# Joining two column-split pieces of a chunk on TensorE, from the fifth chunk on, with the instruction order planned anew

## The chip, the cores and the metric

The kernel runs on one core of a Trainium2 chip. The metric is the device time of one execution in microseconds (us), taken as the median of several runs. TensorE (PE in the profile) does the matrix products, VectorE (DVE) and ScalarE (ACT) the elementwise work and the copies out of PSUM, SyncE (SP) issues the transfers.

## The reference

Three steps follow each other; only their shapes and formulas matter here.

```python
# q, k, v, a_re, a_im: batch 4, 8 heads, 768 tokens, head size 48
for t in range(S):                       # a gated linear recurrence
    S_re, S_im = ar*S_re - ai*S_im + kv, ar*S_im + ai*S_re
    y[:, :, t] = einsum('bhd,bhde->bhe', q[:, :, t], S_re)
...
x = y as 3072 tokens x 384
h = x @ w_in; x = (h * clip(h + 3, 0, 6) / 6) @ w_out        # 384 -> 2048 -> 384
h = ((x @ w1) * (x @ w2)) @ w3; return h @ w_out2            # 384 -> 1024 -> 1024 -> 384
```

## The kernel before, in words

The recurrence is done in 24 chunks of 128 tokens, six for each of the four batch entries; `u` counts them from 0. Two chunks make a group, whose gates, angles and scaled keys and queries are prepared by ScalarE and VectorE (`group`). Four chunks (two in each of the first two cases) make a block of 512 tokens (256), and for each block the first network's two layers run on TensorE: `s1` (lines 742 to 744 with output `x`, nine matmuls of 512 columns each for one slice of 128 hidden units) and `s2` (the same lines with output `m`). After the last block come the folding of two weights (lines 1042 to 1044) and the second network.

One chunk (`chunk`) issues on TensorE:

- `tr`, two times three transposes (line 684), whose results ScalarE copies into the tile `Ks`. The first chunks of a batch entry and the later ones alike do this, but the last chunk of a batch entry (u = 5, 11, 17, 23) doesn't, as nobody needs the state after it;
- `sc`, two times four products of keys with queries (line 693), masked by VectorE into the tiles `P0` and `P1`;
- `pv`, the products of V with the masked scores (line 705) and, except in the first chunk of a batch entry, of the state `A` with the queries (line 710), into the PSUM tile `py`, which ScalarE copies to `ys`. `ys` goes by transfers into `xf` and is split by ScalarE (`xh`) and VectorE (`xl`) into the input of `s1`;
- `upd`, the products of V with `Ks` (line 722), into the PSUM tile `pt`, copied by ScalarE to `ut`. It is left out in the last chunk of a batch entry;
- `turned_`, four transposes of `ut` (line 731), after which VectorE forms the next state `A` in two steps (one in the first chunk of a batch entry).

`pv` and `upd` use the array in two halves of 64 columns (`tile_position=(0, 64 * j)`, shown as 128\*64 and 96\*64 in the profile). All other matmuls use it whole. In the traces each of these float32 products counts as two matmul instructions, so `upd` is 16 of them, `pv` 16 in the first chunk of a batch entry and 32 in the others.

Nothing is ordered by hand. Every step is handed to a planner (`Plan`) with an estimated duration, what it reads and writes, and for some steps a due time (`pins`). The planner works the due times backwards (`o.due`), then simulates the engines: whichever engine is free first takes, among its steps whose inputs and buffers are ready, the one due earliest. The order that comes out is the program's order on each engine. Buffers are few: one `Ks`, one `Kc`, one each of `KT`, `QT`, `P0`, `P1`, and five PSUM slots named `x`, shared by `tr`, `sc`, `pv`, `upd`, `turned_` and the outputs of `s1`. `xh` and `xl` exist once, so the next block's input can be written only after the last `s1` of the block before. `FILL`, `UB`, `MB`, `hold` and other constants were set for the order before and stay as they are.

Of the kernel before, what the change touches and what calls it, by code (L numbers as in the profile page):

```python
# [45 lines left out]


class Op:
    __slots__ = ("i", "eng", "dur", "fn", "deps", "succ", "due", "bufs", "end", "table", "nd", "ready", "pin", "lat", "boost", "size", "until")


class Plan:
# [21 lines left out]
        self.slots.setdefault(tag, n)  # L74
        return Buf(tag, make, free, key)

    def add(self, eng, dur, fn, r=(), w=(), table=None, pin=None, lat=None, part=False, boost=0.0, size=0, until=None):
        o = Op()
        o.size, o.until = size, until
        o.i, o.eng, o.dur, o.fn, o.table, o.pin, o.boost = len(self.ops), eng, dur, fn, table, pin, boost + self.bias  # L80
        o.lat = self.LAT if lat is None else lat
        deps = set()
        for b in r:
            deps.update([] if b.part else b.writers)
        for b in w:
            deps.update(b.readers if not b.part else [])
            if not part and not b.part:
                deps.update(b.writers)
        for b in r:
            b.readers.append(o)  # L90
        for b in w:
            if part or b.part:
                b.writers.append(o)
            else:
                b.writers, b.readers = [o], []
        o.bufs = list(dict.fromkeys([b for b in list(r) + list(w) if b.tag is not None]))
        for b in o.bufs:
            b.left += 1
        o.deps, o.succ = deps, []
        for d in deps:  # L100
            d.succ.append(o)
        self.ops.append(o)
        return o

    def run(self, swap, engines=("PE", "ACT", "DVE", "SP", "POOL"), window=48, switch=1.3, hold=4.0, first=None):
        ops = self.ops
        for o in reversed(ops):
            late = o.pin if o.pin is not None else 1e9
# [14 lines left out]
        freed = {t: [] for t in self.slots}  # L123
        held = set()
        table, bus, cols = first, 0.0, {}
        if first:
            swap(first)
        order = []
# [28 lines left out]
        while len(order) < n:  # L157
            e = min((x for x in engines if lists[x]), key=lambda x: free[x])
            now = free[e]
            for o in [x for x in lists[e][:400] if x.until is not None and now >= x.until]:  # L160

                lists[e].remove(o)
                o.end = now
                n -= 1
                done.add(o)
                for b in o.bufs:
                    b.left -= 1
                    if b.left == 0 and b in held:
                        freed[b.tag].append(now + 0.37)
                        freed[b.tag].sort()  # L170
                        bisect.insort(events, now + 0.37)
            if not lists[e]:
                continue
            best, bk, soon = None, None, None
            cnt = 0
            for o in lists[e]:
                if cnt >= window and best is not None:
                    break
                cnt += 1
                if any(d not in done for d in o.deps):  # L180
                    continue
                at = fits(o, now)
                if at is None:
                    continue
                for d in o.deps:
                    at = max(at, d.end + self.gap(d, o))
                key = o.due - o.boost
                if o.table and o.table != table:
                    key += hold
                if at > now + 1e-9:  # L190
                    if soon is None or at < soon:
                        soon = at
                    continue
                if bk is None or key < bk:
                    best, bk = o, key
            if best is None:
                at = bisect.bisect_right(events, now + 1e-9)
                nxt = events[at] if at < len(events) else None
                if soon is not None and (nxt is None or soon < nxt):
                    nxt = soon  # L200
                if nxt is None:
                    parked.add(e)
                    if len(parked) == sum(1 for x in engines if lists[x]):
                        raise RuntimeError("no instruction can go on")
                    free[e] = 1e9
                else:
                    free[e] = nxt
                continue
            o = best
            lists[e].remove(o)  # L210
            if o.table and o.table != table:
                now += switch
                swap(o.table)
                table = o.table
            o.end = now + o.dur
            if e == "PE":
                left, t0 = o.dur, now
                while left > 1e-9:
                    k = int(t0 / TICK + 1e-9)
                    rate = 1.0 if cols.get(k - 1, 0) >= 3060 else 0.5  # L220
                    d = min(left / rate, (k + 1) * TICK - t0)
                    cols[k] = cols.get(k, 0) + d * rate * 2400
                    left -= d * rate
                    t0 += d
                o.end = t0
            for x in parked:
                free[x] = o.end
            parked.clear()
            bisect.insort(events, o.end)
            for g in {self.gap(o, x) for x in o.succ}:  # L230
                bisect.insort(events, o.end + g)
            if o.size:
                bus = max(bus, o.end + 0.65) + o.size / 300e3
                o.lat = bus + 1.55 - o.end
            free[e] = o.end
            for b in o.bufs:
                if b not in held:
                    held.add(b)
                    if b.key:
                        pos[b.key] += 1  # L240
                    if taken[b.tag] < self.slots[b.tag]:
                        taken[b.tag] += 1
                    else:
                        freed[b.tag].pop(0)
                b.left -= 1
                b.end = max(b.end, o.end + (o.lat if o.lat > 1 else 0.0))
                if b.left == 0:
                    at = b.end + (0.37 if b.tag.startswith("ps") else self.LAT)
                    freed[b.tag].append(at)
                    freed[b.tag].sort()  # L250
                    bisect.insort(events, at)
            done.add(o)
            order.append(o)
            o.fn()


def c_act(n, psum=False):
    return n / 1200.0 + (0.05 if psum else 0.095)
# [161 lines left out]
def main_kernel(tc, q, k, v, a_re, a_im, w_in, w_out, w1, w2, w3, w_out2, consts, qT, kT, arT, aiT, vT, wiT, woT, w1T, w2T, w3T, wo2T, out, blocks=(2, 2, 4, 4, 4, 4, 4)):  # L420
# [12 lines left out]
    for n in blocks:  # L433
        blk.append((u0, n))
        u0 += n
    GT = 2
    FILL = (20, 38.1, 10, 52.8, 16, 52.7)
    FIRST_GROUPS = ((0, 2), (2, 2), (4, 2))
    groups = [(b, c0, n) for b in range(B) for c0, n in (FIRST_GROUPS if b == 0 else ((0, 2), (2, 2), (4, 2)))]
# [5 lines left out]
    with tc.tile_pool(name="keep", bufs=1) as kp:  # L445
      c5_ = kp.tile([128, 2, 128], F32, name="c2")
      flag = kp.tile([1, 1], I32, name="flag")
      with ctx:
# [44 lines left out]
        def ACT(dur, fn, r, w, **kw):  # L493
            return P.add("ACT", dur, fn, r, w, **kw)
# [4 lines left out]
        def PE(dur, fn, r, w, **kw):  # L499
            return P.add("PE", dur, fn, r, w, **kw)  # L500
# [4 lines left out]
        def A(o, i, f, scale=1.0, bias=0.0, **kw):  # L505
            act.activation(out=o, in_=i, func=f, scale=scale, bias=bias, **kw)  # L506
# [161 lines left out]
        def chunk(u, c_, Kc, KT, QT, ys, mt):  # L668
# [32 lines left out]
            def pv():  # L701
                for p in range(4):
                    for j in range(2):
                        h = 2 * p + j
                        pe.matmul(py()[64 * j:64 * j + 64, p, :], vb.ap[:, h, :], Pm[h // 4]()[:, h % 4, :],  # L705
                                  start=True, stop=first, tile_position=(0, 64 * j), skip_group_check=True)
                    if not first:
                        for j in range(2):
                            h = 2 * p + j
                            pe.matmul(py()[64 * j:64 * j + 64, p, :], Ap.ap[:, h, :], QT()[:, h, tok],  # L710
                                      start=False, stop=True, tile_position=(0, 64 * j), skip_group_check=True)
            PE(0.1 + 4 * 0.22 * (1 if first else 2), pv, [vb, QT] + Pm + ([] if first else [Ap]), [py, seen[u]])
            ACT(c_act(512, True), lambda: A(ys()[:, :, c_, :], py(), AF.Copy), [py], [ys], part=True)
            if not last:

                pt = PS("x", [128, 4, 96], 5, 1)
# [2 lines left out]
                def upd():  # L719
                    for p in range(4):  # L720
                        for j in range(2):
                            pe.matmul(pt()[64 * j:64 * j + 64, p, :], vb.ap[:, 2 * p + j, :], Ks()[:, 2 * p + j, :],
                                      start=True, stop=True, tile_position=(0, 64 * j), skip_group_check=True)
                PE(4 * 0.17 + 0.02, upd, [Ks, vb], [pt])
                ACT(c_act(384, True), lambda: A(ut(), pt(), AF.Copy), [pt], [ut])
                pu = PS("x", [96, H, 64], 5, 1)
                An = At[u % 2]
# [488 lines left out]
```

## Time and profile before

| | |
|---|---|
| median of three runs | 925.55 us (924.24 to 926.18) |
| the profiled execution's own time | 924.97 us |
| its span, first to last instruction | 922.8 us |
| PE busy | 880.2 us (95%) |
| DVE busy, ACT busy | 586.0 us (63%), 508.8 us (55%) |
| mean granted TensorE clock | 0.998 of full speed |

The span is 2.2 us shorter than the execution's own time. TensorE first works at 27.82 us, when the first group's keys are ready, and is busy for nine tenths or more of each of the page's 40 slices of the span from the fourth to the last but one.

### The profile page before, as it was taken

Reading aid. Unit: us, or ns where it says so; the run is one execution under the profiler, and the core shown is the slowest. Engines: PE = TensorE matmul, PEld = TensorE weight load, DVE = VectorE, ACT = ScalarE, POOL = GpSimd, SP = SyncE. Lnnn points to the kernel's source line nnn. Section 1 sums busy time; section 2 is a strip of 40 time slices with the busy share of each in tenths; the row PEclk is TensorE's granted clock in tenths of the full one; section 3 lists DMA queues with packets and bytes.
Section 4 is the critical chain, followed back from the end, with each engine's and each line's share of the span. In section 5 each row is a group of like instructions: output and inputs, shape, how many; then the busy total and the mean of one; then the engine's idle time right before and its main releaser. Section 6 shows DMA issues by size and latency. Waiting matters only on the chain.

```text
span 922.8 us, 13306 instructions
## 1 busy us (share of the span) xinstructions
PE 880.2 (95%) x5194; PEld 759.2 (82%) x5194; DVE 586.0 (63%) x913; ACT 508.8 (55%) x816; POOL 0.2 (0%) x4
## 2 busy tenths in 40 slices
PE   0689999999999999999999999999999999999997
PEld 0578989888888888878888888898989888898987
DVE  6999999889998787869453699663223232313131
ACT  7999888978887567656523566453222222212130
POOL 0000000000000000000000000000000000000000
PEclk9999999999999999999999999999999999999999
DMA  6894736357581645365325666230101000000001
GB/s 267 214 251 157 197 107 169 96 128 169 159 208 47 152 145 149 81 143 160 98 47 126 204 234 247 92 92 23 60 9 52 18 21 26 5 32 0 35 1 38
DMA packets 55991, 102.88 MB, mean 111 GB/s; under 512 B 6384, under 2 KB 34160, under 8 KB 55920
## 3 DMA queue, kind: packets, MB, share of 16 engines
q1 hardware_dynamic: 55920, 101.94, 38.8%
q8 instruction: 43, 0.70, 0.3%
q14 instruction: 28, 0.23, 0.1%
HBM read 64.62 MB, written 13.63 MB: 85 GB/s over the span
## 4 chain that ended last, share of the span: by engine, by line
PE 75%; ACT 11%; DVE 11%; DMA 1%; issue 1%; SPq 1%; ACTq 0%; DVEq 0%
PE x L742 12%; PE x L743 12%; PE x L744 12%; PE m L742 5%; PE m L743 5%; PE m L744 5%; PE m L1112 4%; PE x L693 4%; PE m L1110 4%; PE m L1111 4%; ACT u L506 3%; ACT W L506 3%; ACT L1146 2%; PE x L705 2%; DVE gl L509 1%; PE x L710 1%
## 5 line engine op out<-in xcount | busy, mean ns | idle before, releaser
L506 ACT ACTIVATE r<-x 128x512 f32<-128x512 f32 (+1 forms) x144 | 82.1, 571 | 88.4 <-PE x L744 64.6
L506 ACT ACTIVATE gh<-r 128x512 fp32r<-128x512 f32 (+1 forms) x108 | 64.2, 596 | 98.1 <-PE m L744 68.5
L742 PE MATMUL m<-gh,W 128*128 128x512 f32 (+1 forms) x288 | 110.1, 382 | 0.5 <-ACT gh L506 0.5
L743 PE MATMUL m<-gl,W 128*128 128x512 f32 (+1 forms) x288 | 107.7, 374 | 1.1 <-DVE gl L509 1.0
L744 PE MATMUL m<-gh,W 128*128 128x512 f32 (+1 forms) x288 | 107.2, 372 | 0.0
L509 DVE TENSOR_TENSOR gl<-r,gh 128x512 fp32r<-128x512 f32 (+1 forms) x108 | 70.0, 648 | 52.3 <-ACT gh L506 50.9
L509 DVE TENSOR_TENSOR r<-r,x 128x512 f32<-128x512 f32 x48 | 33.0, 688 | 103.0 <-PE x L744 103.0
L742 PE MATMUL x<-xh,W 128*128 128x512 f32 x240 | 96.3, 401 | 0.0
L743 PE MATMUL x<-xl,W 128*128 128x512 f32 x240 | 93.7, 390 | 0.0
L744 PE MATMUL x<-xh,W 128*128 128x512 f32 x240 | 93.6, 390 | 0.0
L742 PE MATMUL x<-W 128*128 128x512 f32 (+1 forms) x228 | 84.6, 371 | 0.0
L744 PE MATMUL x<-W 128*128 128x512 f32 (+1 forms) x228 | 83.6, 367 | 0.0
L743 PE MATMUL x<-W 128*128 128x512 f32 (+1 forms) x228 | 83.6, 367 | 0.0
L881 DVE SCALAR_TENSOR_TENSOR r<-r,x 128x512 f32<-128x512 f32 (+1 forms) x96 | 61.0, 637 | 13.0 <-ACT r L506 12.5
L506 ACT ACTIVATE W<-W 128x768 f32<-128x768 f32 (+3 forms) x78 | 64.5, 848 | 5.1 <-DMA W<-in_w3T_dram 2.5
L743 PEld LDWEIGHTS m<-gl,W 128*128 128x128 f32 x288 | 54.3, 188 | 11.3 <-DVE gl L509 2.5
L742 PEld LDWEIGHTS m<-gh,W 128*128 128x128 f32 x288 | 54.2, 188 | 11.0 <-issue 0.9
L744 PEld LDWEIGHTS m<-gh,W 128*128 128x128 f32 x288 | 54.2, 188 | 9.5
L742 PEld LDWEIGHTS x<-xh,W 128*128 128x128 f32 x240 | 45.1, 188 | 10.2 <-issue 0.9
L744 PEld LDWEIGHTS x<-xh,W 128*128 128x128 f32 x240 | 45.1, 188 | 9.7
L743 PEld LDWEIGHTS x<-xl,W 128*128 128x128 f32 x240 | 45.1, 188 | 8.5
L506 ACT ACTIVATE u<-u 128x768 f32<-128x768 f32 x60 | 50.3, 838 | 0.4
(233 smaller groups left out, 1867.0 us busy)
## 6 DMA issues: line engine op xcount, KB each, us to landing
KT<-Kc SPq DMA_DIRECT2D x72, 129.0 KB, 3.6
QT<-cs SPq DMA_DIRECT2D x72, 128.0 KB, 4.6
W<-in_w3T_dram SPq DMA_DIRECT2D x16, 512.0 KB, 4.3
v<-in_vT_dram SPq DMA_DIRECT2D x24, 256.0 KB, 2.8
W<-in_wiT_dram SPq DMA_DIRECT2D x8, 768.0 KB, 6.8
W<-in_woT_dram SPq DMA_DIRECT2D x8, 768.0 KB, 6.5
ar<-in_arT_dram SPq DMA_DIRECT2D x12, 384.0 KB, 3.4
ai<-in_aiT_dram SPq DMA_DIRECT2D x12, 384.0 KB, 3.3
```

Source lines behind the costliest of these rows:

```text
L506: act.activation(out=o, in_=i, func=f, scale=scale, bias=bias, **kw)
L509: dve.tensor_tensor(out=o, in0=i0, in1=i1, op=op)
L693: pe.matmul(p_()[:, i, :], KT()[:, 4 * g + i, tok], QT()[:, 4 * g + i, tok])
L705: pe.matmul(py()[64 * j:64 * j + 64, p, :], vb.ap[:, h, :], Pm[h // 4]()[:, h % 4, :], start=True, stop=first, tile_position=(0, 64 * j), ...
L742: pe.matmul(o, wh, xh, start=start, stop=False, **kw)
L743: pe.matmul(o, wh, xl, start=False, stop=False, **kw)
L744: pe.matmul(o, wl, xh, start=False, stop=stop, **kw)
L881: DVE(c_tt(n), lambda: dve.scalar_tensor_tensor(out=r()[:, :n], in0=r()[:, :n], scalar=6.0, in1=h()[:, :n], op0=ALU.min, op1=ALU.mult), [h ...
L1110: pe.matmul(o(), g[1]()[:, a], Wb()[:, 0, i % 2], start=(i == 0), stop=False)
L1111: pe.matmul(o(), g[1]()[:, a], Wb()[:, 1, i % 2], start=False, stop=False)
L1112: pe.matmul(o(), g[2]()[:, a], Wb()[:, 0, i % 2], start=False, stop=(i == KI - 1))
L1146: P.run(lambda t_: act.preload_act_table_set(t_), window=48, hold=3.94, first=EXP_SET)
```

## The change

From the fifth chunk on (`JOINED = 4`), and where the chunk has an `upd`, `pv` and `upd` are added to the plan as one step of TensorE whose duration is the sum of both and which reads and writes what both do. That holds for 16 chunks: u = 4, 6 to 10, 12 to 16 and 18 to 22. The matmuls themselves stay as they were. The copy of `py` is now added after the step with `upd` in program text. The planner also learns a cost: whenever TensorE goes from a step in halves (`cols=True`) to one with the whole array or back, its simulated clock is charged `turn=0.17` us. As both alter the simulation, the order of all engines is set anew.

```diff
-    def add(self, eng, dur, fn, r=(), w=(), table=None, pin=None, lat=None, part=False, boost=0.0, size=0, until=None):
+    def add(self, eng, dur, fn, r=(), w=(), table=None, pin=None, lat=None, part=False, boost=0.0, size=0, until=None, cols=False):
...
             if e == "PE":
-                left, t0 = o.dur, now
+                left, t0 = o.dur + (turn if o.cols != halves else 0.0), now
+                halves = o.cols
...
+    JOINED = 4
...
-            PE(0.1 + 4 * 0.22 * (1 if first else 2), pv, [vb, QT] + Pm + ([] if first else [Ap]), [py, seen[u]])
-            ACT(c_act(512, True), lambda: A(ys()[:, :, c_, :], py(), AF.Copy), [py], [ys], part=True)
+            pvd, pvr, pvw = 0.1 + 4 * 0.22 * (1 if first else 2), [vb, QT] + Pm + ([] if first else [Ap]), [py, seen[u]]
+            if last or u < JOINED:
+                PE(pvd, pv, pvr, pvw, cols=True)
...
-                PE(4 * 0.17 + 0.02, upd, [Ks, vb], [pt])
+                if u < JOINED:
+                    PE(4 * 0.17 + 0.02, upd, [Ks, vb], [pt], cols=True)
+                else:
+                    PE(pvd + 4 * 0.17, lambda: (pv(), upd()), pvr + [Ks], pvw + [pt], cols=True)
+            ACT(c_act(512, True), lambda: A(ys()[:, :, c_, :], py(), AF.Copy), [py], [ys], part=True)
+            if not last:
                 ACT(c_act(384, True), lambda: A(ut(), pt(), AF.Copy), [pt], [ut])
```

## Rows read from the trace of the kernel before

**Rows 1.** Busy time by stretch: start:end, length, then each engine's busy us.

```profile
0.00:64.00 64.00, 30.74 (x215) 24.49 (x216) 54.08 (x83) 57.35 (x80) 0.20 (x4) 1.00 0.80 247
64.00:169.00 105.00, 102.62 (x830) 93.19 (x830) 101.88 (x166) 94.16 (x158) 0.00 (x0) 1.00 0.59 157
169.00:258.00 89.00, 88.76 (x569) 73.79 (x569) 82.78 (x128) 73.71 (x116) 0.00 (x0) 1.00 0.58 145
258.00:917.00 659.00, 657.89 (x3586) 567.69 (x3584) 346.64 (x538) 283.54 (x466) 0.00 (x0) 1.00 0.30 87
```

**Rows 2.** Timeline of TensorE, an update alone: start, duration, line, operation.

```profile
291.26 0.40 PE L744 MATMUL m<-gh,W 128*128 128x512 f32 x1
291.59 0.88 PE L722 MATMUL x<-Ks,v 128*64 128x96 f32 x16
292.40 0.50 PE L742 MATMUL x<-xh,W 128*128 128x512 f32 x1
292.73 0.39 PE L743 MATMUL x<-xl,W 128*128 128x512 f32 x1
```

**Rows 3.** Timeline of TensorE, an update right behind products with V.

```profile
284.13 0.39 PE L744 MATMUL m<-gh,W 128*128 128x512 f32 x1
284.45 1.09 PE L705 MATMUL x<-P,v 128*64 128x128 f32 x16
285.37 0.83 PE L722 MATMUL x<-Ks,v 128*64 128x96 f32 x16
286.13 0.50 PE L742 MATMUL x<-xh,W 128*128 128x512 f32 x1
286.47 0.40 PE L743 MATMUL x<-xl,W 128*128 128x512 f32 x1
```

**Rows 4.** Timeline of TensorE, products with V alone.

```profile
410.05 0.40 PE L744 MATMUL x<-xh,W 128*128 128x512 f32 x1
410.37 1.09 PE L705 MATMUL x<-P,v 128*64 128x128 f32 x16
411.40 0.50 PE L742 MATMUL m<-gh,W 128*128 128x512 f32 x1
411.73 0.39 PE L743 MATMUL m<-gl,W 128*128 128x512 f32 x1
```

**Rows 5.** Timeline of TensorE, updates and a product with V at other places.

```profile
104.76 0.88 PE L722 MATMUL x<-Ks,v 128*64 128x96 f32 x16
...
204.55 0.83 PE L722 MATMUL x<-Ks,v 128*64 128x96 f32 x16
...
421.04 0.44 PE L705 MATMUL x<-P,v 128*64 128x128 f32 x4
...
452.47 0.88 PE L722 MATMUL x<-Ks,v 128*64 128x96 f32 x16
...
466.78 0.88 PE L722 MATMUL x<-Ks,v 128*64 128x96 f32 x16
...
501.06 0.83 PE L722 MATMUL x<-Ks,v 128*64 128x96 f32 x16
```

**Rows 6.** Timelines of TensorE and ScalarE, from chunk 22 to chunk 23.

```profile
499.25 0.44 PE L705 MATMUL x<-P,v 128*64 128x128 f32 x4
...
501.27 0.60 ACT L506 ACTIVATE ys<-x 128x512 f32<-128x512 f32 x1 [3.47 <-PE x L710]
501.93 0.49 ACT L506 ACTIVATE ut<-x 128x384 f32<-128x384 f32 x1
...
506.33 0.44 PE L705 MATMUL x<-P,v 128*64 128x128 f32 x4
```

**Rows 7.** Timelines of TensorE and VectorE, passage to the last block.

```profile
510.45 0.40 PE L742 MATMUL m<-gh,W 128*128 128x512 f32 x1
...
518.17 0.96 DVE L509 TENSOR_TENSOR xl<-xf,xh 128x768 fp32r<-128x768 f32 x1
...
520.66 0.39 PE L742 MATMUL x<-xh,W 128*128 128x512 f32 x1
```

More of the change, by code (lines that the diff above doesn't have):

```diff
@@ L48 @@
 class Op:
-    __slots__ = ("i", "eng", "dur", "fn", "deps", "succ", "due", "bufs", "end", "table", "nd", "ready", "pin", "lat", "boost", "size", "until")
+    __slots__ = ("i", "eng", "dur", "fn", "deps", "succ", "due", "bufs", "end", "table", "nd", "ready", "pin", "lat", "boost", "size", "until", "cols")
 class Plan:
@@ L75, in buf @@
         return Buf(tag, make, free, key)
-    def add(self, eng, dur, fn, r=(), w=(), table=None, pin=None, lat=None, part=False, boost=0.0, size=0, until=None):
+    def add(self, eng, dur, fn, r=(), w=(), table=None, pin=None, lat=None, part=False, boost=0.0, size=0, until=None, cols=False):
         o = Op()
-        o.size, o.until = size, until
+        o.size, o.until, o.cols = size, until, cols
         o.i, o.eng, o.dur, o.fn, o.table, o.pin, o.boost = len(self.ops), eng, dur, fn, table, pin, boost + self.bias
@@ L103, in add, with run @@
         return o
-    def run(self, swap, engines=("PE", "ACT", "DVE", "SP", "POOL"), window=48, switch=1.3, hold=4.0, first=None):
+    def run(self, swap, engines=("PE", "ACT", "DVE", "SP", "POOL"), window=48, switch=1.3, hold=4.0, first=None, turn=0.17):
         ops = self.ops
@@ L125, in run @@
         table, bus, cols = first, 0.0, {}
+        halves = False
         if first:
```

## The prediction

> **What bounds the kernel now.** I read the busy time by stretch first, then TensorE's waits, the chain of waits, and last the timeline around every small piece that a chunk puts between the long matmuls. By stretch, TensorE is busy all but 0.24 us of the 89 us from 169 to 258 us and all but 1.11 us of the 659 us from 258 to 917 us; in the 105 us before that it lacks 2.38 us, and 33.26 us in the first 64 us, where the first groups are being prepared [rows 1]. So from 169 us on the end is set by how much work TensorE has, and a step of TensorE that gets shorter should move the end by as much. From 64 to 169 us another engine is about as full: VectorE is busy for 101.88 of 105 us [rows 1], and the chain of waits runs there mostly over VectorE and ScalarE. Time saved on TensorE in that stretch may only become idle time.
>
> In the timeline, the reader is to look at starts, not at durations: matmuls overlap, so what a piece costs is what it pushes back the start of the long matmuls behind it. At the passage to the last block, 45 long matmuls stand between 510.45 and 520.66 us [rows 7], which is 10.21 / 45 = 0.227 us from start to start. Two such steps are 0.454 us.
>
> **What joining saves.** An update that stands alone among long matmuls stretches the two steps from the long matmul before it to the second one behind it from 0.454 us to 292.73 - 291.26 = 1.47 us: it costs 1.02 us [rows 2]. Products with V alone, in a first chunk, cost 411.73 - 410.05 - 0.454 = 1.23 us [rows 4]. Both together, the update right behind, cost 286.47 - 284.13 - 0.454 = 1.89 us [rows 3]. The update inside a pair thus costs 1.89 - 1.23 = 0.66 us, and a joint pair saves 1.02 - 0.66 = 0.36 us against two separate pieces. The 0.36 us is what it takes to enter and to leave the halves once: the sixteen instructions run just as long.
>
> How often? Sixteen chunks are joined. In the old order four of their updates already stand right behind products with V, the first at 204.55 and the last at 501.06 us; the other twelve, from 104.76 to 466.78 us, don't [rows 5]. The first of the four follows another chunk's products, but in number of turns that is the same. So twelve turns in and out vanish: 12 x 0.36 = 4.3 us of TensorE's work. Three of the twelve lie before 169 us (chunks 4, 6 and 7), where VectorE is the fuller engine. If these are worth nothing, 9 x 0.36 = 3.2 us remain. These are the two ends; as TensorE still was busy for 102.62 of the 105 us there [rows 1], it is not wholly without effect, but the chain of waits leaves it out. I take 3.5 us, nearer to the lower end.
>
> **What else moves.** No instruction is added or taken away on any engine and no transfer changes, so ScalarE, VectorE and SyncE have the same work in another order. The charge of 0.17 us for a turn emits nothing. It puts the planner's estimate for a lone update, 0.70 us before, at 1.04 us, close to the 1.02 us measured [rows 2], so its picture of TensorE gets better; but the constants around it stay, and I count no gain for that.
>
> The joint step needs the masked scores, the old state and `Ks` all at once. Before, an update needed only `Ks` and could run well ahead of its chunk's products. That has two consequences. First, the state now passes through TensorE in series: products and update, copy to `ut`, transposes, two steps of VectorE, next products. One such link already stands in the trace between chunks 22 and 23: from 499.25 to 506.33 us, 7.08 us [rows 6]. Three links for the four chunks of a block make 21 us, while a block's `s1` and `s2` have 2 x 16 x 9 = 288 long matmuls of 0.227 us, 65 us, so the links can be hidden behind `s1` and `s2` as long as the planner begins a block's chunks that early. It should, since due times are worked backwards through the longer chain. Second, `Ks` is single: the transposes of the next chunk now wait for the joint step before, and `Kc` is free for the next group only after them. Late in the kernel VectorE is far from full (346.64 of 659 us [rows 1]) and has room for this. At the blocks' ends it is even helped: chunk 19's update ran at 452.47 us, 31 us behind its products at 421.04 us [rows 5], and now its transposes must come sooner, which frees `Kc` sooner. I cost both at nothing. If the cover is gone, the price is what the next block waits, given below.
>
> The copies out of PSUM are where a rule speaks against the change. In the link above the copy to `ys` stands ahead of the copy to `ut` on ScalarE, 501.27 and 501.93 us, and the second waits some 0.6 us for the first [rows 6]. If every joint step paid that on the path that ends last, 16 x 0.6 = 9.6 us would be lost, and the time would be 924.97 - 3.5 + 9.6 = 931 us. The Trainium skill, page TensorEngine Tiling (Array Packing), section PSUM Bottleneck, says that using the array in parts makes TensorE faster but not the emptying of PSUM, which can then be what limits. By that rule the joint step, which fills two PSUM tiles in a row, would be paced by ScalarE. The trace bears it out for the link but not for the end: TensorE went on with long matmuls, and between 258 and 917 us it lacks 1.11 us in all [rows 1]. I take zero for it.
>
> **The new order** has a price that no row shows. All small stalls of the old order from 64 to 917 us add up to 2.38 + 0.24 + 1.11 = 3.7 us [rows 1]. A new order may have half as many or twice as many, so from 1.9 us less to 3.7 us more; I take none. The first 64 us depend little on TensorE and hold none of the joint steps.
>
> **Sum.** The profiled execution took 924.97 us. 924.97 - 3.5 = 921.5 us. The median of the runs is 0.58 us above the profiled one, so in terms of that median I expect 922.0 us.
>
> **Rivals.**
> *The gain goes into new stalls.* The twelve turns vanish, but the new order stands in the way of itself by about as much, say 2 to 4 us: 924 to 926 us. For it: the constants fit the old order, which has only 3.7 us of stalls after 64 us. Against it: the planner sees every buffer and every dependency, and most of the time it has backlog to choose from. A measurement of this kernel can tell about 0.2% from no change, 1.85 us.
>
> *Slower: a passage between blocks runs dry.* `xh` is single, so the next block's input is split only after the last `s1` of the old one, and TensorE lives on held-back `s2` meanwhile: 45 matmuls, five slices of 2.04 us, to 520.66 us, while the last `xl` starts at 518.17 and ends at 519.13 us [rows 7]. There are some 1.5 us to spare. At two passages, after chunks 15 and 19, the update with its PSUM tile, its copy, its transposes and its two steps of VectorE used to come well after the passage (452.47 us [rows 5]) and is now ahead of it. PSUM slots and engine time held there may leave fewer slices of `s2` in hand. One slice fewer at both beyond the spare time costs up to 4.1 us and eats the gain; two fewer cost 8.2 us and give 924.97 - 3.5 + 8.2 = 929.7 us. From one and a half on the kernel is slower than before. Against it: what the passage loses in transposes of chunk 19, which used to fill it, it gains in the update.
>
> *ScalarE's copies pace the joint steps*, as worked out above: 931 us. That would also be slower.
>
> *The order also gets better*: 4.3 us of turns and 1.9 us of stalls, 918.8 us, with the planner's better picture for a cause.
>
> **How the numbers follow.** The forecast, a gain of 1.9 to 5 us, gets 0.55. The better order, more than 5 us, gets 0.08. The gain lost to stalls, within 1.85 us of the old time, gets 0.22. A dry passage gets 0.12 and pacing by ScalarE 0.03. So faster has 0.63, same 0.22, slower 0.15. The forecast alone spans 920.5 to 923.7 us. The range starts at the better order, 918.8 us, and takes in the case of no gain up to 1.35 us above the old median, 926.9 us; slower cases and a still better order are left out, under 0.2 together.
>
> **What would show it.** Updates in the profile after should stand right behind their own products sixteen times, and a pair should cost 0.66 us more than products alone. The TensorE work between 169 us and the last chunk should shrink by 3 us or so, and the products of chunk 23, at 506.33 us before [rows 6], should start 3 to 4 us earlier, with everything behind them. Idle time of TensorE from 64 to 917 us should stay near 3.7 us. If it grows by more than 2 us, the place where it grows tells the rival: between 64 and 169 us it is VectorE's stretch, at the start of a block it is a dry passage, and a wait of `turned_` for ScalarE's copy is the pacing. The prediction is wrong if the four passages get longer than they were, or if the first product of chunk 4 already comes later than before.

## The result and the profile after

The change made the kernel slower: 934.35 us median of six runs (931.56 to 936.64) against 925.41 us, a ratio of 1.0097 (95% interval 1.0077 to 1.0116), 9.0 us. I had forecast 922.0 us and a range up to 926.9 us.

The joint step does what was forecast of it. The timeline of TensorE in the kernel after, around the joint step of chunk 12 (start, duration, line, operation):

```profile
286.31 0.39 PE L753 MATMUL x<-xh,W 128*128 128x512 f32 x1
286.62 1.09 PE L708 MATMUL x<-P,v 128*64 128x128 f32 x16
287.55 0.83 PE L726 MATMUL x<-Ks,v 128*64 128x96 f32 x16
288.31 0.50 PE L751 MATMUL m<-gh,W 128*128 128x512 f32 x1
288.64 0.40 PE L752 MATMUL m<-gl,W 128*128 128x512 f32 x1
```

From 286.31 to 288.64 us are 2.33 us, less two long steps of 0.227 us 1.88 us, as for a pair in the old order [rows 3]; such a pair now stands in all sixteen chunks. Counted over the whole trace, TensorE enters the halves 27 times, before 39 times: the twelve turns are gone. But the time went elsewhere. The same profile by stretch (busy time of TensorE, its weight loads, VectorE, ScalarE and GpSimd, granted clock, transfers):

```profile
0.00:64.00 64.00, 27.35 (x190) 21.12 (x191) 54.02 (x81) 57.10 (x78) 0.20 (x4) 0.95 0.80 248
64.00:169.00 105.00, 100.91 (x811) 92.18 (x810) 100.88 (x163) 93.52 (x158) 0.00 (x0) 1.00 0.56 157
169.00:258.00 89.00, 88.80 (x591) 75.70 (x590) 81.39 (x128) 68.76 (x109) 0.00 (x0) 1.00 0.55 140
258.00:917.00 659.00, 654.55 (x3558) 564.68 (x3557) 347.50 (x542) 287.39 (x472) 0.00 (x0) 1.00 0.30 87
```

Set beside [rows 1]: TensorE's idle time grew from 33.26 to 36.65 us in the first 64 us, from 2.38 to 4.09 us up to 169 us, fell from 0.24 to 0.20 us up to 258 us, and grew from 1.11 to 4.45 us up to 917 us. Together that is 8.4 us more, in a span that grew by 7.7 us (930.5 us); 3.4 us of it lie in the first 64 us, where no joint step stands yet.

Where along the way? Block starts tell it: the first `s1` matmul of the third, fourth and last block, in the timelines of TensorE, after and then before:

```profile
174.42 0.40 PE L751 MATMUL x<-xh,W 128*128 128x512 f32 x1
...
263.86 0.50 PE L751 MATMUL x<-xh,W 128*128 128x512 f32 x1 [1.09 <-ACT xh L509]
...
528.28 0.39 PE L751 MATMUL x<-xh,W 128*128 128x512 f32 x1
```

```profile
169.43 0.40 PE L742 MATMUL x<-xh,W 128*128 128x512 f32 x1
...
258.07 0.39 PE L742 MATMUL x<-xh,W 128*128 128x512 f32 x1
```

The third block starts 5.0 us late, the fourth 5.8 us, the last 7.6 us [rows 7]; behind that nothing more is lost. In the stretch from the third to the last block nine turns were to save 3.2 us, and it became 2.6 us longer.

Two places hold most of it. The first lies ahead of 64 us, as the timelines of TensorE show, before and then after:

```profile
53.38 1.46 PE L868 MATMUL x<-xh,W 128*128 128x256 f32 x6
...
56.83 2.76 PE L868 MATMUL x<-xh,W 128*128 128x256 f32 x12
...
60.96 1.56 PE L899 MATMUL m<-gh,W 128*128 128x256 f32 x6
...
63.92 1.46 PE L868 MATMUL x<-xh,W 128*128 128x256 f32 x6
65.22 1.03 PE L899 MATMUL m<-gl,W 128*128 128x256 f32 x4
```

```profile
55.64 0.52 PE L687 MATMUL x<-c,Kc 128*128 128x128 f32 x3 [2.28 <-DVE Kc L512]
...
59.31 1.55 PE L726 MATMUL x<-Ks,v 128*64 128x96 f32 x16 [2.26 <-ACT Ks L509]
60.79 2.93 PE L877 MATMUL x<-xh,W 128*128 128x256 f32 x6
```

In the old order the first block's `s1` (256 columns; line 868, after the change 877) fills the waits for chunk 2's transposes and copies. In the new order it stands behind chunk 2's update: TensorE waits for 2.28 and 2.26 us, with nothing in the order to fill the gaps. By 64 us TensorE has started 6 of the first block's 192 matmul instructions, before 25 (counted in the whole traces); the six from 63.92 to 65.22 us are 0.217 us apart, so the 19 are some 4.1 us of work (an estimate). That work doesn't come back: the second block starts at 97.03 us, before at 97.05 us, but 18 matmuls of the first are still behind it. From there to the third block's start, when both kernels have done the same work, TensorE lacks 4.29 us, before 2.38 us. The 18 matmuls (3.9 us) and 1.9 us more idle time, less three turns (1.1 us), make 4.7 us of the 5.0 us.

The second place is the passage to the fourth block. TensorE runs dry there and then works at half clock:

```profile
260.66 0.50 PE L752 MATMUL m<-gl,W 128*128 128x512 f32 x1 [0.66 <-DVE gl L512]
...
263.86 0.50 PE L751 MATMUL x<-xh,W 128*128 128x512 f32 x1 [1.09 <-ACT xh L509]
264.87 0.62 PE L752 MATMUL x<-xl,W 128*128 128x512 f32 x1 [0.51 <-DVE xl L512]
265.29 0.63 PE L753 MATMUL x<-xh,W 128*128 128x512 f32 x1
```

The brackets are idle time of 2.3 us in all, and what ended it. From 264.87 to 268.28 us the long matmuls start 0.43 us apart, not 0.227, and these eight steps cost 1.6 us more. By stretch (columns as above), the granted clock of 0.50 from 266 to 268 us is the lower level of 1.2 GHz:

```profile
266.00:268.00 2.00, 2.00 (x6) 1.54 (x6) 2.00 (x4) 1.87 (x3) 0.00 (x0) 0.50 0.98 276
```

The series chain shows too, for example between the products of chunks 4 and 5, in the stretch where VectorE is full:

```profile
117.83 0.44 PE L708 MATMUL x<-P,v 128*64 128x128 f32 x4
...
138.72 0.44 PE L708 MATMUL x<-P,v 128*64 128x128 f32 x4
```

From products to products are 20.9 us, as the steps between them wait in full queues. In the old order, where the update of chunk 4 stood ahead of its products at 104.76 us [rows 5], they were 8.2 us, from 120.41 to 128.61 us. So chunk 5 comes ten us late, though chunk 4 comes 2.6 us early. But TensorE had other work meanwhile: all its idle time from 97 us to the third block is 1.9 us more than before, as above.

Three theories, then. Theory 1: the joint step puts the state's chain in series, and that costs. Theory 2: the planner's charge for a turn spoils the order. Theory 3: neither in particular; any new order loses under constants that were set for the old one.

### The profile page after: what moved, and what is told of

Its sections match the earlier page's. It is cut to its first block, busy times and chain, and to the rows that moved or that the text cites. A ratio compares the mean times of both kernels' runs of the same rounds, so it can differ in the third digit from the quotient of the medians.

```text
span 930.5 us, 13276 instructions
## 1 busy us (share of the span) xinstructions
PE 879.6 (95%) x5188; PEld 761.4 (82%) x5188; DVE 584.6 (63%) x913; ACT 507.3 (55%) x816; POOL 0.2 (0%) x4
## 4 chain that ended last, share of the span: by engine, by line
PE 74%; ACT 13%; DVE 7%; DMA 3%; issue 1%; SPq 1%; DVEq 0%; ACTq 0%
PE x L751 13%; PE x L752 12%; PE x L753 12%; PE m L751 5%; PE m L752 5%; PE m L753 5%; ACT u L509 4%; PE m L1121 4%; PE m L1120 4%; PE m L1119 4%; ACT W L509 3%; PE x L696 3%; ACT L1155 2%; PE x L708 2%; PE x L713 1%
```

## The experiments

Times are medians. Ratios are against the kernel before, measured beside each, with their 95% intervals; a loss or gain in us is worked out from the ratio, so it can differ a little from the difference of medians. Where a run is said to be late at a block, that comes from its one profile.

**Each half of the change alone.** Joining without the charge:

```diff
-hold=4.0, first=None, turn=0.17):
+hold=4.0, first=None, turn=0.0):
```

> Joined steps from chunk 4, but the planner charges nothing for a turn, so its order is the old one up to the first joint step. Theory 1 (the joint step puts the state's chain in series through TensorE and delays the products of chunk 5 and the third block): third block starts near 174 us as after the whole change, total 930 to 936 us. Theory 2 (the charge for turns moves the planner's clock against the set constants, so the fillers end too early, TensorE stands still near 52 to 59 us and its clock falls to half): no half clock ahead of 64 us, third block near 169 us, total 920 to 924 us.

Measured: 942.81 us, ratio 1.0197 (1.0176 to 1.0217). The charge without joining:

```diff
-    JOINED = 4
+    JOINED = 99
```

> No joint step anywhere, but the planner charges 0.17 us for a turn. Theory 1 (series chain): close to the kernel before, 924 to 927 us. Theory 2 (the charge spoils the order of the first 170 us): half clock between 56 and 64 us, third block near 174 us, total 930 to 936 us.

Measured: 938.36 us, ratio 1.0142 (1.0119 to 1.0165). Each half alone loses more than both together, 18.2 and 13.1 us against 9.0 us. Both totals lie above what either theory had expected of them. As the only cause, theory 2 falls with the first run and theory 1 with the second: neither half is needed for a loss.

Each half loses at places of its own, though. With the charge alone, TensorE's order is that of the whole change up to 87 us; joined without the charge, it is the old one up to 79 us. By stretch, the charge alone and then joining alone:

```profile
60.00:64.00 4.00, 2.71 (x19) 2.31 (x20) 4.00 (x6) 3.97 (x6) 0.00 (x0) 0.50 1.01 266
60.00:64.00 4.00, 2.93 (x25) 1.91 (x23) 3.36 (x5) 4.00 (x10) 0.00 (x0) 1.00 1.06 255
```

The first block's `s1` starts at 62.76 us with the charge alone and at 54.36 us with joining alone, against 60.79 us after the whole change and 53.38 us before. So what the whole change loses ahead of 64 us comes with the charge, as theory 2 had it. Joining alone loses later: its third block starts 4.1 us late and its fourth 16.3 us. The line that adds the copy of `py` has moved in both halves; it has moved in the faster runs below as well.

**Joined later.** `JOINED = 8` in place of 4.

> The change as it is, but joined only from chunk 8 on, so chunks 4, 6 and 7 keep two separate steps. Theory 1 (series chain in the stretch where VectorE is full): third block back at 169 to 170 us, total 4 to 5 us under the whole change, 928 to 930 us. Theory 2 (charge): third block stays near 174 us, total 932 to 936 us.

Measured: 937.40 us, ratio 1.0134 (1.0104 to 1.0164). The third block starts at 170.97 us, 3.5 us earlier than with the whole change, which looks like theory 1. But 18 `s2` matmuls of the second block (0.12 us each, 2.2 us) are still left at that start, and none after the whole change, so only 1.3 us are won. The fourth block starts 9.7 us late, and the total is no better than with the whole change and above both expectations of 928 to 930 and 932 to 936 us.

**The price of a turn.** The order of before, and in the middle of sixteen updates one short product with the whole array:

```diff
...
                     for p in range(4):
+                        if p == 2 and u >= 4:
+                            pe.matmul(pt()[:, 384:416], ident, vb.ap[:, 0, :32], start=True, stop=True, skip_group_check=True)
...
```

> The kernel before in its own order, with one short product over the whole array (32 columns, into unused PSUM columns) in the middle of the 16 updates from chunk 4 on, which adds 16 turns out of the halves and back and nothing else. If a turn in and out costs 0.36 us of the path that ends last: 16 x 0.36 = 5.8 us and 16 x some 0.05 us for the products themselves, 931 to 933 us in all; with the three turns before 169 us hidden 930 us. If turns are mostly hidden: under 1 us more than before.

Measured: 931.89 us, ratio 1.0080 (1.0064 to 1.0097), 7.4 us or 0.46 us for each turn with its product. The timeline of TensorE in that kernel, one such update:

```profile
294.41 0.39 PE L747 MATMUL m<-gh,W 128*128 128x512 f32 x1
294.73 0.55 PE L725 MATMUL x<-Ks,v 128*64 128x96 f32 x8
295.21 0.41 PE L723 MATMUL x<-v,c 128*128 128x32 f32 x2
295.55 0.55 PE L725 MATMUL x<-Ks,v 128*64 128x96 f32 x8
296.03 0.50 PE L745 MATMUL x<-xh,W 128*128 128x512 f32 x1
296.36 0.40 PE L746 MATMUL x<-xl,W 128*128 128x512 f32 x1
```

1.95 us from the long matmul ahead to the second behind, against 1.47 us for a lone update [rows 2]: 0.48 us more. Sixteen of these are 7.7 us, and 7.4 us (5.9 to 9.0) came out at the end. Work on TensorE does move the end, and 0.36 us for a turn fits if the short product itself costs the other 0.12 us, where I had expected 0.05 us. Three of the sixteen stand ahead of the third block, which starts 1.5 us late; single profiles of an unchanged order differ there by 0.5 us.

**A nudge without any change of work.** Twice the kernel before, without joint steps and without a charge, with one duration estimate of the planner altered:

```diff
-    return n / 1200.0 + (0.05 if psum else 0.095)
+    return n / 1200.0 + (0.05 if psum else 0.096)
```

> The kernel before without joint steps and without a charge for turns; only the planner's estimate for a ScalarE step without PSUM is 1 ns longer. No engine's work changes, but the order comes out new. Theory 3 (any new order under constants set for the old one costs some 5 to 15 us, joint step or not): 929 to 937 us. Theory 1 (the joint step's series chain is what costs): within 2 us of the kernel before.

Measured: 933.93 us, ratio 1.0092 (1.0077 to 1.0108).

```diff
-                PE(4 * 0.24, sc, [KT, QT], [p_, m_])
+                PE(4 * 0.24 - 0.01, sc, [KT, QT], [p_, m_])
```

> The same with another nudge: only the planner's estimate for the score products on TensorE is 10 ns shorter. Theory 3: 928 to 936 us, by another path than with the ScalarE nudge. Theory 1: within 2 us of the kernel before.

Measured: 933.65 us, ratio 1.0092 (1.0076 to 1.0107). This is the control that decides: an estimate that is off by one ns costs about as much as the whole change. A new order is enough for such a loss, without a joint step and without a charge, as theory 3 says. Where the loss sits differs. In the profile of the 1 ns nudge the third and fourth blocks start 0.8 and 0.4 us earlier than before and the fifth 8.5 us late. The longest wait lies at the passage to the fifth; busy time by stretch, and the wait from the timeline:

```profile
344.00:353.00 9.00, 6.22 (x39) 5.09 (x38) 8.43 (x14) 7.09 (x14) 0.00 (x0) 0.88 0.52 166
```

```profile
351.03 1.55 PE L722 MATMUL x<-Ks,v 128*64 128x96 f32 x16 [2.78 <-ACT Ks L506]
```

TensorE stands still for 2.78 us ahead of an update whose `Ks` isn't copied yet, and what follows starts at a lower clock (the update takes 1.55 us, alone in the old order 0.88 us [rows 2]). With the 10 ns nudge the third block is already 4.5 us late, and the products of chunks 4 and 5 are 21.8 us apart, as far as after the whole change, though nothing is joined:

```profile
120.55 0.44 PE L705 MATMUL x<-P,v 128*64 128x128 f32 x4
...
142.37 0.44 PE L705 MATMUL x<-P,v 128*64 128x128 f32 x4
```

**Turns saved in the old order.** The updates of chunks 7, 10, 16 and 21 and their copies are emitted right behind the next products with V; all else stays in its place.

```diff
-            PE(0.1 + 4 * 0.22 * (1 if first else 2), pv, [vb, QT] ...
+            PE(0.1 + 4 * 0.22 * (1 if first else 2), lambda: (pv(), [f() for f in late], late.clear()), [vb, QT] ...
-                PE(4 * 0.17 + 0.02, upd, [Ks, vb], [pt])
+                PE(4 * 0.17 + 0.02, (lambda: (pt(), late.append(upd))) if u in (7, 10, 16, 21) else upd, [Ks, vb], [pt])
```

> The old order kept, but the updates of chunks 7, 10, 16 and 21 (with their copies to ut) are issued right behind the next products with V on TensorE, where nothing in between needs them: four turns in and out fewer, nothing else moved. If a turn is worth 0.36 us of the path that ends last: 4 x 0.36 = 1.4 us less than before, 1.1 us if chunk 7's is hidden; ratio 0.9985 to 0.9988. If turns saved are not gained: ratio 1.000.

Measured: 926.35 us, ratio 1.0016 (1.0007 to 1.0025): 1.5 us slower, where 1.1 to 1.4 us less was expected. The turns did go (TensorE enters the halves 35 times in place of 39, and its busy time fell from 880.2 to 878.1 us), but waits came in their place, two of them of `turned_` for the copy:

```profile
237.00 0.53 PE L734 MATMUL x<-c,ut 128*96 128x128 f32 x3 [0.59 <-ACT ut L506]
...
475.58 0.42 PE L734 MATMUL x<-c,ut 128*96 128x128 f32 x2 [0.59 <-ACT ut L506]
```

These two are 1.2 us; what else ate the gain was not followed up. That an update moved back takes the slack from what follows it, where a planner would have put other work, is argued and not shown.

**Joint steps where the order fits them.** Without the charge, so that the old order stands for longer (on TensorE up to 238 us), and with the chunks as a set, picked by the planner's own clock:

```diff
-    JOINED = 4
+    JOINED = (13, 14, 15, 16, 20, 21, 22)
...
-            if last or u < JOINED:
+            if last or u not in JOINED:
...
-                if u < JOINED:
+                if u not in JOINED:
```

> Joint steps only in chunks 13, 14, 15, 16, 20, 21 and 22, no charge for turns, so that the old order stands up to chunk 12 (block passages of the first 258 us unchanged). Of the seven, the updates of 13, 15, 16, 20 and 21 stood alone before: five turns in and out fewer. The set was picked as one for which the planner's own clock ends no later than with the old order. Theory 3 (the joint step itself gains its turns, and the change lost by the order alone): 5 x 0.36 = 1.8 us less than before, up to 3 us with a slightly better order, ratio 0.997 to 0.998. Theory 1 (the series chain costs wherever it stands): 2 us or more above the kernel before.

Measured: 924.06 us, ratio 0.9987 (0.9978 to 0.9996). And with the set `(10, 12, 13, 14, 15, 20, 21, 22)`:

> The same with another set, chunks 10, 12 to 15 and 20 to 22; updates 10, 13, 15, 20 and 21 stood alone, again five turns fewer. Theory 3: 1.8 us less than before, up to 2.7 us, ratio 0.997 to 0.998. Theory 1: 2 us or more above it.

Measured: 923.14 us, ratio 0.9982 (0.9973 to 0.9991). Both are faster than the kernel before, by 1.2 and 1.7 us with bounds from 0.4 to 2.5 us. The first gained less than the 1.8 us of its five turns. The second gained about the 1.8 us expected, but its order differs from 212 us on and its trace has seven turns fewer, not five, which would be worth 2.5 us. The joint step by itself does no harm in these blocks, which contradicts theory 1 there: in the second kernel chunk 11's products start 13.2 us behind those of chunk 10, as after the whole change, and the fourth block starts 0.9 us early. By stretch, that kernel:

```profile
169.00:258.00 89.00, 88.93 (x570) 74.16 (x570) 83.31 (x127) 69.51 (x114) 0.00 (x0) 1.00 0.61 154
```

TensorE is kept as full as in the old order up to 258 us; the profiled span is 920.4 us against 922.8 us.

**The half clock ahead of 64 us.** In the kernel after, TensorE has 13 fillers, before 16, and a granted clock of 0.61 and 0.54 from 56 to 64 us, by stretch:

```profile
56.00:60.00 4.00, 1.39 (x13) 1.00 (x13) 4.00 (x6) 3.98 (x8) 0.00 (x0) 0.61 1.01 338
60.00:64.00 4.00, 4.00 (x22) 3.10 (x19) 3.27 (x4) 3.99 (x7) 0.00 (x0) 0.54 1.14 179
```

Filler matmuls (results that nobody reads, to keep TensorE busy) that the planner doesn't know of, twelve ahead of chunk 2's transposes and twelve ahead of its update:

```diff
...
+                        if u == 2 and a == 0:
+                            for _ in range(12):
+                                pe.matmul(junk()[:, :256], ident, c5.ap[:, :2].rearrange("p a b -> p (a b)"), skip_group_check=True)
...
```

> The whole change with its order, and 24 filler matmuls more that nobody reads (256 columns, ident by the constants), twelve ahead of chunk 2's transposes and twelve ahead of its update, where TensorE stood idle for 2.28 and 2.26 us and its clock then was at half until 64 us. If the half clock ahead of 64 us is on the path: 1.5 to 2.5 us under the whole change, 932 to 933 us. If VectorE and ScalarE set the pace there anyway: same as the whole change within 1 us.

Measured: 935.81 us, ratio 1.0128 (1.0112 to 1.0143). That is neither of the two outcomes expected. The fillers were too many; chunk 2's update came at 64.31 us, 5.0 us later than in the kernel after. So once more with `range(5)`:

> As the run with 24 fillers, whose fillers took 5.3 us each dozen where TensorE stood idle for 2.3 us and so came to stand in the way themselves: now five and five, some 2.2 us each, which just fill the two gaps ahead of chunk 2's transposes and update. If the half clock ahead of 64 us is on the path: full clock in 52 to 64 us and 1.5 to 2.5 us under the whole change, 932 to 933 us. If VectorE and ScalarE set the pace there: full clock there and the same as the whole change within 1 us.

Measured: 932.49 us, ratio 1.0085 (1.0069 to 1.0101). The clock is full from 52 to 64 us, the third block starts at 173.49 us in place of 174.42 us, and the span of the profiled run is 930.3 us against 930.5 us. By the ratios it is 1.1 us under the whole change, but with bounds (worked out from both intervals) from 1.2 us worse to 3.4 us better, so this doesn't decide whether the half clock costs anything at the end. It also tests the clock alone: the fillers don't do the work that the order put off, and by 64 us 13 of the first block's matmuls have started, against 25 before.

**Joint steps with constants fitted anew.** No charge, joint steps in nine chunks, and the constants altered: shifts by group from the sixth group on, bonuses from the third block on, due times from the fourth:

```diff
+    JOINED = (8, 9, 13, 14, 15, 16, 19, 20, 22)
...
-        UB = (23.1, 3.6, 0, 0, 10.9, 5.2)
+        UB = (23.1, 3.6, 0, 0, 10.9, 5.2, 1.32, 0.5, -4.42, 4.83, 0.39, -2.14)
...
-                pins["2", j, f] = t_ + 4.09 * sl
+                pins["2", j, f] = t_ + (4.09, 4.09, 4.09, 4.43, 6.15, 4.26, 4.8)[j] * sl
...
```

> Joint steps in chunks 8, 9, 13 to 16, 19, 20 and 22, no charge for turns, and the planner's constants (shifts by group and chunk stage, bonus and due times by block) fitted anew from the fifth group on, for an order that its own clock ends earlier. Six lone updates (8, 13, 15, 16, 19, 20) lose their turns: 6 x 0.36 = 2.2 us. Theory 3 (order and constants are one fit, the joint step itself gains): 2 to 4 us less than before, ratio 0.996 to 0.998. Theory 1 (the series chain costs wherever it stands): no better than before.

Measured: 923.21 us, ratio 0.9980 (0.9971 to 0.9989), 1.8 us faster (1.0 to 2.7), as much as the set of eight and a little under the 2 to 4 us expected; its trace has five turns fewer, not the six counted on. The whole change, sixteen joint steps with the charge, was not run with constants set anew.

## Why the prediction was wrong

The step that failed is "The new order has a price": I took none, bounded it by the old order's stalls, 1.9 us less to 3.7 us more, and held that the first 64 us depend little on TensorE. The change cost 9.0 us although its twelve turns went, so with the 4.3 us of the turns the new order cost some 13 us (an estimate: 9.0 + 4.3). The charge alone cost 13.1 us, the two nudges 8.5 us each. All five other orders that were new from the early chunks on with the old constants lost 8.5 to 18.2 us. The old order's 3.7 us of stalls were no measure for this: they are what was left after the constants had been set for that order, and a nudge gives that up. In this change the charge put the first block's `s1` behind chunk 2's update, and 19 matmuls, some 4.1 us of TensorE's work, were behind by 64 us; the passage to the fourth block cost 2.3 us of idle time and 1.6 us at half clock. How the loss divides between the charge and the joint steps as a whole stays open, as either alone lost more.

Point by point. The saving of 0.36 us a turn and the count of twelve stand: the pair costs the same after, sixteen extra turns fit the price, and joint steps where the order fits them gave 1.2 to 1.8 us, no more than their turns. That turns ahead of 169 us may be worth nothing was not tested by itself. "No instruction is added or taken away" missed that the planner sets the number of fillers: three are gone. The sign that I had named, a later first product of chunk 4, didn't come: it starts at 117.83 us, before at 120.41 us, and the loss was there all the same. Two others did: TensorE's idle time from 64 to 917 us grew from 3.7 to 8.7 us, and the products of chunk 23 start at 514.00 us, 7.7 us later than before and not 3 to 4 us earlier.

The series chain was costed at nothing. From products to products it took 20.9 us between chunks 4 and 5 and 21.4 us between chunks 22 and 23, where I had measured 7.08 us. But links as long stand in the old order itself (22.7 us between chunks 12 and 13), in a nudge that joins nothing and in the faster set of eight (20.0 us between chunks 21 and 22), and most of the third block's 5.0 us was lost ahead of chunk 4; what share the chain has stays open. The rival of a dry passage was right in kind: 2.3 us of idle time at the passage to the fourth block, followed by half clock, and a like one in the 1 ns nudge; it came after chunk 11, though, and not after chunks 15 and 19 for PSUM slots as I had argued. The rival "the gain goes into new stalls" was right in kind and far too small. The better planner's picture of a turn was no help.

Pacing by ScalarE's copies didn't show: `turned_` waits for `ut` twice in the kernel after, 1.4 us in all, before twice for 1.6 us, and two waits of 0.59 us came up when updates were moved by hand. The Trainium skill, page TensorEngine Tiling (Array Packing), section PSUM Bottleneck, says that tiling speeds up TensorE but not the emptying of PSUM, so that after a fourfold speedup the copy out of PSUM may become the bottleneck; no run here shows that at the end of the kernel.

## What to carry to other kernels

Where a program orders the instructions, a change of its estimates or steps is two changes: the work, and a new order. Run a nudge that alters no work as a control before the difference is put down to the work; here 1 ns cost 8.5 us, five times the 1.7 us that joint steps won where the order suited them. And judge such an edit with its constants set anew, or where the old order can stand. To find where an order loses, count how much of a fixed list of work is done by a given time: the start of a block can come on time while work of the block before is left over.

## What the runs showed that I had not expected

An order can cost through TensorE's clock as well: after idle time at a passage the long matmuls started 0.43 us apart in place of 0.227 us, at a granted clock of 0.50. Giving the full clock back from 52 to 64 us with fillers left the end about where it was (932.49 us), as fillers keep the clock but do none of the work put off. The runs after the change also spread more, 931.56 to 936.64 us in six, where the kernel before stayed within 923.73 and 926.53 us.
